# Splitting a second layer's output weights ahead of time and parking them in device memory

## The chip, the cores and the metric

The kernel runs on one core of a Trainium2 chip. The metric is device time in microseconds of one launch; the time before is a median of three runs. The profile shows one further execution of the same program.

## The reference, cut to what matters

Two batches of 12-head attention (448 positions, 64 wide) with a mixing of heads before and after the softmax, then two dense layers on the 896 tokens that come out of it. `w_out` of the second layer is the matrix whose handling changes.

```python
scores = scale * q @ k.T ; scores = einsum('bhij,hg->bgij', scores, w_pre)
attn   = softmax(scores) ; attn   = einsum('bhij,hg->bgij', attn, w_post)
x = (attn @ v) laid out as (896, 768)
h = x @ moe_w_in                       # 768 -> 2048
x = (h * clip(h + 3, 0, 6) / 6) @ moe_w_out      # 2048 -> 768
h = x @ moe2_w_in
P = a0 + a1*h + a2*h**2 + a3*h**3
Q = 1 + |b0|*|h| + |b1|*h**2
out = (P / (Q + 1e-6)) @ moe2_w_out
```

The weights arrive as float64. They are turned into float32 on the chip, and every product is made of three float32r matmuls (high times high, high times low, low times high), so each operand is split into a high part (`h`) and a low part (`l`).

## The kernel before, in words

**Attention, 0 to about 240 us.** The queries go in eight chunks (four for each batch) of 12, 12, 12 and 9 steps; a step handles ten query rows of all heads. The order of each step is written out by hand: `premix` (three matmuls into `M`, then a maximum on VectorE and an exponential on ScalarE), `postmix` of two steps before (eight matmuls into `A`), and at set steps either `scores` of the next chunk (twelve matmuls) or `av_unit`, attention times values of the chunk before (32 matmuls into `X` in a step that has two units). The tables `SST`, `QST` and `AVST` say which step of a chunk holds what. `scores` are evicted into `stg` tiles and moved ("spread") into the layout of the mix, `full`, by twelve DMAs a head pair's worth at a time (line 250). GpSimd splits each `full` slice (`gsplit`, lines 287 and 289) two steps before it is used, and the first split of a chunk needs every spread of that chunk. `load_v` (line 132) fetches values three or four head pairs ahead into four `vraw` buffers. All these DMAs are issued by SyncE (SP), in program order. The keys of batch two (`load_k`, line 126; three DMAs of 448 KB) and their splits (`k_prep`: a ScalarE cast on line 234, a VectorE subtraction on line 235 a step later) are put into chunk 2, the third. `kraw` and `stg` share the five buffers of the tag `raw`.

**Layer 1, about 240 to 475 us.** Written in order, but from here on a planner in the framework reorders the instructions of each engine by its own cost model, within the dependencies. Meanwhile ten slices of the second layer's `w_in` are converted and parked in device memory (`pre`, line 713), to be fetched back in layer 2 (line 398).

**Layer 2, first half, about 475 to 644 us.** For each of 16 slices `f` of the 2048 hidden units: `gemm_in` for tokens 0 to 383 (part 0) and for tokens 384 to 895 (part 1), six steps of three matmuls each; the rational function `act2` on part 0 and its split into `g0`; then the product of slice `f - 1` with `w_out` (`gemm_out0`, 18 matmuls) into six PSUM banks. Part 1 of a slice is kept in `g1[f]`: with `act2` done at once for four slices (`f % 4 == 3`), only copied for the twelve others (`late_f`). A slice of `w_out` is loaded as raw float64 (`wraw`, two buffers), converted (`to_f32`: ScalarE line 419, VectorE lines 421, 423 and 427) into its own place in `wo2`, which holds all 16, and split (`wh`, `wl`, lines 451 and 452).

**Layer 2, second half, about 644 to 720 us.** Part 1 times `w_out`, 16 slices of 24 matmuls (four blocks of 128 tokens, two halves of the columns): 384 matmuls. `prep(i)` splits `g1[f]` (lines 773 and 774) and splits the slice of `w_out` once more, out of `wo2` (lines 844 and 845). `act2` of the twelve late slices runs here as well. The last two slices are kept for the end (`TAIL`), where each bank is finished, evicted and stored.

Of the kernel before, what the change touches and what calls it, by code (L numbers as in the profile page):

```python
# [7 lines left out]
F32 = mybir.dt.float32  # L8
F32R = mybir.dt.float32r
I32 = mybir.dt.int32  # L10
AF = mybir.ActivationFunctionType
ALU = mybir.AluOpType
# [14 lines left out]
NP = H // 2  # L27
# [21 lines left out]
def fused_kernel(  # L49
# [15 lines left out]
    nc = tc.nc  # L65
# [30 lines left out]
    PRE2 = list(range(2, 12))  # L96
    dram = ctx.enter_context(tc.tile_pool(name="dram", bufs=1, space=bass.MemoryType.DRAM))
    pre = {f: dram.tile([128, KD * 128], F32, name=f"pre{f}") for f in PRE2}

    xp = tc.alloc_tile_pool(name="xp", bufs=1)  # L100
    x1p = tc.alloc_tile_pool(name="x1p", bufs=1)
# [22 lines left out]
    def load_k(b, m):  # L124
        t = front.tile([128, 2, S], F32, tag="raw", bufs=5, name=f"kraw{b}_{m}")
        nc.sync.dma_start(out=t, in_=k[b, :, 2 * m : 2 * m + 2])
        kraw[(b, m)] = t
# [102 lines left out]
    def k_prep(b, hp):  # L230
        src = kraw[(b, hp // 2)][:, hp % 2, :]
        hi, lo = kst[:, 0, hp, :], kst[:, 1, hp, :]
        preps.append([
            lambda: nc.scalar.activation(out=hi, in_=src, func=AF.Copy),
            lambda: nc.vector.tensor_tensor(out=lo, in0=src, in1=hi.bitcast(F32), op=ALU.subtract),
        ])
# [151 lines left out]
        if f >= GLAG:  # L388
            units.append(("out2", f - GLAG, 0))
    raws, spl = {}, {}  # L390
    wo2 = []
    ucur = [0, 0]

    def load_unit(u, eng=nc.sync):
# [37 lines left out]
    def split_pieces(u):  # L432
        t, n = raws.pop(u)
        n *= 128
        if u[0] == "in2" and u[1] in pre:
            w = t
        else:
            if u[0] == "out2":
                if not wo2:
                    wo2.append(pools["gp2"].tile([128, KF, DM], F32, name="wo2"))  # L440
                w = wo2[0][:, u[1], :]
            else:
                w = pools["late"].tile([128, KD * 128], F32, tag="wf", bufs=2, name="wf")[:, :n]
            yield from to_f32(t, n, w)
        hv = pools["late"].tile([128, KD * 128], F32R, tag="wh", bufs=3, name="wh")[:, :n]
        lv = pools["late"].tile([128, KD * 128], F32R, tag="wl", bufs=3, name="wl")[:, :n]
        if u[0] in ("in1", "out1"):
            nc.gpsimd.tensor_scalar(out=hv, in0=w, scalar1=1.0, scalar2=0.0, op0=ALU.mult, op1=ALU.add)  # L448
            nc.gpsimd.tensor_tensor(out=lv, in0=w, in1=hv.bitcast(F32), op=ALU.subtract)  # L449
        else:  # L450
            nc.scalar.activation(out=hv, in_=w, func=AF.Copy)
            nc.vector.tensor_tensor(out=lv, in0=w, in1=hv.bitcast(F32), op=ALU.subtract)  # L452
        if u[0] != "out2":
            hv, lv = (x.rearrange("p (a b) -> p a b", b=128) for x in (hv, lv))
        spl[u] = (hv, lv)

# [14 lines left out]
    def advance(i):  # L471
        load_units(i + 2)
        split_units(i + 1)
# [35 lines left out]
    def gemm_in(p, hp, w):  # L509
        t0, t1 = PARTS[p]  # L510
        wh, wl = w
        for c in range(KD):
            yield mm3(hp[:, : t1 - t0], wh[:, c, :], wl[:, c, :], XH[:, c, t0:t1], XL[:, c, t0:t1], c == 0, c == KD - 1)
# [5 lines left out]
    def run(g):  # L519
        for _ in g:  # L520
            pass
# [35 lines left out]
    for C, (b, r0, n, G) in enumerate(chunks):  # L557
# [3 lines left out]
        def add(units, steps):  # L561
            for i, u in enumerate(units):
                sched.setdefault(steps[i * len(steps) // len(units)], []).append(u)
# [3 lines left out]
        if C + 2 < len(chunks):  # L567
            add([lambda: q_prep(C + 2, 0, NP // 2), lambda: q_prep(C + 2, NP // 2, NP)], QST[G])
        if C == NCH - 2:
            add([lambda m=m: load_k(1, m) for m in range(3)], [4, 5, 6])  # L570
            add([lambda h=h: k_prep(1, h) for h in range(NP - 1)], [8, 8, 9, 10, 11])
        if C == NCH - 1:
            add([lambda: k_prep(1, NP - 1)], [0])
        if C > 0:
            add([lambda h=h: av_unit(C - 1, h) for h in range(1, H, 2)], [("av", a) for a in (AVST[G] if nxt is not None else AVLAST)])

# [173 lines left out]
    def bank2(tag, name):  # L750
        return pm.tile([128, 512], F32, tag=tag, name=name)
# [36 lines left out]

    acc0 = []
    g0, g1 = {}, {}  # L790
    late_f = [f for f in range(KF) if f % 4 != 3]

    def gemm_out0(f):
        w = spl.pop(("out2", f, 0))
# [5 lines left out]
    for f in range(KF):  # L800
        advance(ui)
        w = spl.pop(("in2", f, 0))
        tags = (f"a{2 - f}0", f"a{2 - f}1") if f < GLAG else ("h0", "h1")
        g1[f] = gp.tile([128, P1], F32, tag=f"g1_{f}", name=f"g1_{f}")
        hp = bank2(tags[0], f"h2_{f}_0")
        run(gemm_in(0, hp, w))
        t1 = tm("t1", P0)
        act2(hp[:, :P0], t1, P0)
        g0[f] = tuple(gp.tile([128, P0], F32R, tag="g0" + x, bufs=GLAG + 1, name=f"g0{x}{f}") for x in "hl")
        last = split(t1, *g0[f])  # L810
        hp = bank2(tags[1], f"h2_{f}_1")
        run(gemm_in(1, hp, w))
        if f in late_f:
            nc.scalar.activation(out=g1[f], in_=hp[:, :P1], func=AF.Copy)
        else:
            act2(hp[:, :P1], g1[f], P1)
        ui += 1
        if f >= GLAG:
            advance(ui)
            if f == GLAG:  # L820
                acc0 += [[bank2(f"a{t}{i}", f"acc{t}{i}") for i in range(2)] for t in range(NB0)]
            gemm_out0(f - GLAG)
            ui += 1
    for f in range(KF - GLAG, KF):
        advance(ui)
        gemm_out0(f)
        ui += 1


    flat = [x.rearrange("p c t -> p (c t)") for x in (XH, XL)]  # L830
    NSL = 4
    order = [f for f in range(KF) if f not in late_f] + late_f
    gs, ws = {}, {}

    def prep(i):
        if i >= KF:
            return
        f, sl = order[i], i % NSL
        gs[f] = tuple(x[:, sl * P1 : sl * P1 + P1] for x in flat)
        split(g1[f], *gs[f])  # L840
        w0 = NSL * P1 + sl * DM
        ws[f] = tuple(x[:, w0 : w0 + DM] for x in flat)
        hv, lv = ws[f]
        nc.scalar.activation(out=hv, in_=wo2[0][:, f, :], func=AF.Copy)
        nc.vector.tensor_tensor(out=lv, in0=wo2[0][:, f, :], in1=hv.bitcast(F32), op=ALU.subtract)

    with tc.issue_after(last[0].ins), tc.issue_after(last[1].ins):
        prep(0)
        prep(1)
    for t in range(NB0):  # L850
        o = gp.tile([TB, DM], F32, tag="o", bufs=3, name=f"o0_{t}")
        for i in range(2):
            put(acc0[t][i], t, i, o, i)
        nc.sync.dma_start(out=out[t * TB : t * TB + TB, :], in_=o)
    tags = [("h0", "h1")] + [(f"a{t}0", f"a{t}1") for t in range(NB0)]
    acc1 = [[bank2(tags[t][i], f"acc1{t}{i}") for i in range(2)] for t in range(NB1)]
    TAIL = 2
    for i in range(KF - TAIL):
        with tc.issue_after(last[0].ins), tc.issue_after(last[1].ins):
            prep(i + 2)  # L860
            if i < len(late_f):
                f = late_f[i]
                act2(g1[f], g1[f], P1)
        f = order[i]
        for t in range(NB1):
            for j in range(2):
                gemm_out(acc1[t][j], t, j, gs[f], ws[f], i == 0, False)
    for t in range(NB1):
        row = P0 + t * TB
        o = gp.tile([TB, DM], F32, tag="o", bufs=3, name=f"o1_{t}")  # L870
# [61 lines left out]
```

## Time and profile before

| | |
|---|---|
| median of three runs | 725.36 us (724.59 to 727.18) |
| the profiled execution: its time, its span | 725.5 us, 723.8 us |
| TensorE busy | 697.5 us, 96% of the span |
| VectorE, ScalarE, GpSimd busy | 571.9, 425.5, 257.4 us |
| mean granted TensorE clock | 0.990 of full speed |
| DMA, mean | 135 GB/s, 97.65 MB |

The span is the time from the first to the last instruction of the profiled execution; its own time is 1.7 us longer. Matmuls overlap one another in the records, so a busy TensorE is not yet a TensorE at its peak: their starts tell more than their durations.

### The profile page before, as it was taken

The page shows a single profiled execution, that of the slowest core. Times are in us where ns is not written, and L with a number is a line of the kernel's source. Part 1 is how long each engine was busy: PE and PEld are TensorE (multiplying, and loading weights), DVE is VectorE, ACT ScalarE, POOL GpSimd, SP SyncE. Part 2 cuts the span into 40 slices and gives each one's busy share as a digit, 9 for nine tenths or more (in the row PEclk, how much of TensorE's full clock was granted, in tenths as well). Part 3 has the DMA queues.
Part 4 walks back from the last instruction along what each step waited for, and adds up shares of the span by engine and source line. Part 5 has one row for each costly group of instructions (what it writes and reads, how often), then busy time and mean ns, then how long its engine had stood idle before and what let it go on. Part 6 is the DMA issues. An engine that isn't in the chain of part 4 may idle for free.

```text
span 723.8 us, 12235 instructions
## 1 busy us (share of the span) xinstructions
PE 697.5 (96%) x4457; PEld 620.3 (86%) x4457; DVE 571.9 (79%) x947; ACT 425.5 (59%) x869; POOL 257.4 (36%) x255
## 2 busy tenths in 40 slices
PE   5999989999999999999999999999999999999986
PEld 3779878898888888989888888889899999999976
DVE  5566656665657589899988777899998789789996
ACT  4687868777788443434322221166766677589872
POOL 1787745877778234332444444300000000000000
PEclk8899999999999999999999999999999999999999
DMA  6635565556384354454355455354444222010002
GB/s 193 232 99 163 166 163 177 162 145 190 98 247 144 113 171 130 153 157 150 128 173 172 144 182 180 110 196 155 174 140 144 66 92 89 39 65 1 1 1 88
DMA packets 66333, 97.65 MB, mean 135 GB/s; under 512 B 5532, under 2 KB 54496, under 8 KB 66272
## 3 DMA queue, kind: packets, MB, share of 16 engines
q1 hardware_dynamic: 65920, 96.48, 42.5%
q8 instruction: 35, 0.57, 0.3%
q10 hardware_dynamic: 288, 0.37, 0.1%
q0 software_dynamic: 64, 0.01, 0.1%
q14 instruction: 26, 0.21, 0.1%
HBM read 70.81 MB, written 6.68 MB: 107 GB/s over the span
## 4 chain that ended last, share of the span: by engine, by line
PE 43%; DVE 37%; DMA 10%; issue 5%; ACT 3%; POOL 2%; SPq 0%; ACTq 0%; POOLq 0%; DVEq 0%
PE A L334 8%; DVE wf L423 6%; DVE wf L427 6%; PE X L354 5%; PE h L378 4%; PE h L379 4%; PE sc L268 4%; PE h L380 4%; DMA pre<-wf 4%; DVE gl L539 4%; DVE wf L421 3%; PE M L299 3%; DMA vraw<-in_v_dram 3%; PE acc L379 2%; PE M L301 2%
## 5 line engine op out<-in xcount | busy, mean ns | idle before, releaser
L378 PE MATMUL h<-xh,wh 128*128 128x512 f32 (+1 forms) x384 | 141.7, 369 | 0.6 <-DVE u L766 0.6
L380 PE MATMUL h<-xh,wl 128*128 128x512 f32 (+1 forms) x384 | 140.8, 367 | 0.7 <-DVE wl L452 0.7
L379 PE MATMUL h<-xl,wh 128*128 128x512 f32 (+1 forms) x384 | 140.6, 366 | 0.0
L289 POOL TENSOR_TENSOR sl<-full,sh 120x448 fp32r<-120x448 f32 x89 | 103.0, 1157 | 7.4
L303 DVE TENSOR_REDUCE st<-M 120x1 f32<-120x448 f32 x90 | 56.0, 623 | 57.0 <-PE M L301 56.7
L334 PEld LDWEIGHTS A<-wr,e 120*112 120x112 f32 x720 | 86.4, 176 | 7.7 <-ACT wr L318 3.4
L334 PE MATMUL A<-wr,e 120*112 120x120 f32 x720 | 88.9, 266 | 1.6 <-ACT wr L318 1.6
L419 ACT ACTIVATE wf<-wraw 128x768 f32<-128x768 f32 (+1 forms) x40 | 34.1, 864 | 88.8 <-DMA pre<-wf 56.2
L305 ACT ACTIVATE e<-M,st 120x448 f32<-120x448 f32 x90 | 57.1, 635 | 46.5 <-DVE st L303 46.2
L448 POOL TENSOR_SCALAR wh<-wf 128x768 fp32r<-128x768 f32 (+1 forms) x34 | 32.7, 961 | 138.8 <-DVE wf L427 126.3
L380 PEld LDWEIGHTS h<-xh,wl 128*128 128x128 f32 x384 | 72.1, 188 | 10.1 <-DVE wl L452 1.0
L378 PEld LDWEIGHTS h<-xh,wh 128*128 128x128 f32 x384 | 72.1, 188 | 9.0 <-DVE u L766 1.0
L379 PEld LDWEIGHTS h<-xl,wh 128*128 128x128 f32 x384 | 72.1, 188 | 8.0
L287 POOL TENSOR_SCALAR sh<-full 120x448 fp32r<-120x448 f32 x89 | 54.0, 606 | 62.1 <-PE M L300 35.7
L380 PE MATMUL y<-gh,wl 128*128 128x384 f32 x192 | 70.3, 366 | 0.7 <-POOL wl L449 0.7
L378 PE MATMUL y<-gh,wh 128*128 128x384 f32 x192 | 70.4, 366 | 0.0
L379 PE MATMUL y<-gl,wh 128*128 128x384 f32 x192 | 70.2, 366 | 0.0
L449 POOL TENSOR_TENSOR wl<-wf,wh 128x768 fp32r<-128x768 f32 (+1 forms) x34 | 67.6, 1989 | 2.8
L538 ACT ACTIVATE gh<-g 128x384 fp32r<-128x384 f32 (+1 forms) x32 | 18.6, 580 | 60.3 <-DVE g L536 60.0
L338 ACT ACTIVATE at<-A 112x480 f32<-112x480 f32 x90 | 52.2, 580 | 1.8 <-PE A L334 1.8
L421 DVE TENSOR_SCALAR wf<-wf 128x768 int32<-128x768 int32 (+1 forms) x50 | 33.6, 671 | 21.9 <-ACT wf L419 21.9
L299 PE MATMUL M<-sh,wp_h 120*120 120x448 f32 x90 | 41.4, 460 | 5.7 <-DVE sh L287 5.7
(116 smaller groups left out, 1589.5 us busy)
## 6 DMA issues: line engine op xcount, KB each, us to landing
wraw<-in_moe_w_out_dram SPq DMA_DIRECT2D x28, 768.0 KB
wraw<-in_moe_w_in_dram SPq DMA_DIRECT2D x22, 768.0 KB
full<-stg SPq DMA_DIRECT2D x60, 210.0 KB
vraw<-in_v_dram SPq DMA_DIRECT2D x42, 224.0 KB
wpre<-in_moe_w_in_dram SPq DMA_DIRECT2D x10, 768.0 KB
pre<-wf SPq DMA_DIRECT2D x10, 384.0 KB
wf<-pre SPq DMA_DIRECT2D x10, 384.0 KB
full<-stg SPq DMA_DIRECT2D x24, 157.5 KB
```

Source lines behind the costliest of these rows:

```text
L287: eng.tensor_scalar(out=sh[:r], in0=s[:r], scalar1=1.0, scalar2=0.0, op0=ALU.mult, op1=ALU.add)
L289: return eng.tensor_tensor(out=sl[:r], in0=s[:r], in1=sh[:r].bitcast(F32), op=ALU.subtract)
L299: nc.tensor.matmul(mt[:r, :S], lhsT=a[:r, :r], rhs=sh[:r], start=True, stop=False)
L303: nc.vector.tensor_reduce(out=st[:r, 0:1], in_=mt[:r, :S], op=ALU.max, axis=AX.X, negate=True)
L305: nc.scalar.activation(out=e[:r], in_=mt[:r, :S], func=AF.Exp, bias=st[:r, 0:1], accum_out=st[:r, 1:2])
L334: nc.tensor.matmul(av[:, jc], lhsT=e[:r, jc * JP : (jc + 1) * JP], rhs=wr[:r, :, :rr], start=True, stop=True)
L338: lambda: nc.scalar.activation(out=at[C][:, :, :, c0 : c0 + rr], in_=av, func=AF.Copy)
L378: nc.tensor.matmul(o, lhsT=wh, rhs=mh, start=first, stop=False)
L379: nc.tensor.matmul(o, lhsT=wh, rhs=ml, start=False, stop=False)
L380: nc.tensor.matmul(o, lhsT=wl, rhs=mh, start=False, stop=last)
L421: nc.vector.tensor_scalar(out=wi, in0=wi, scalar1=3, scalar2=None, op0=ALU.logical_shift_left)
L449: nc.gpsimd.tensor_tensor(out=lv, in0=w, in1=hv.bitcast(F32), op=ALU.subtract)
```

## The change

1. In the second layer's first half each slice of `w_out` is converted into a `wf` buffer (two of them, shared with `w_in`; `wo2` is gone), split once, used, and both parts are stored in device memory (`wsp`). In the second half they are fetched back (`fetch`) into seven pairs of buffers, six pairs of which are asked for before that half begins. `prep` no longer splits weights.
2. The four slices whose `act2` on part 1 is done at once are 2, 5, 8 and 11 instead of 3, 7, 11 and 15.
3. For slice 0 the first five of six steps of both parts go ahead of the sixth of part 0. At the end of the first half the products of the first two slices for the first block of tokens go ahead of the last `gemm_out0`, and those of the third behind it.
4. In chunk 2 of the attention the three key loads go to steps 6, 7 and 9 instead of 4, 5 and 6; the key splits to steps 9, 10, 10 and 11 and to steps 0 and 1 of the next chunk.

```diff
+    wsp = {f: [dram.tile([128, DM], F32, name=f"w2{x}{f}") for x in "hl"] for f in range(KF)}
...
-            if u[0] == "out2":
-                if not wo2:
-                    wo2.append(pools["gp2"].tile([128, KF, DM], F32, name="wo2"))
-                w = wo2[0][:, u[1], :]
-            else:
-                w = pools["late"].tile([128, KD * 128], F32, tag="wf", bufs=2, name="wf")[:, :n]
+            w = pools["late"].tile([128, KD * 128], F32, tag="wf", bufs=2, name="wf")[:, :n]
...
-        if u[0] != "out2":
+        if u[0] == "out2":
+            for d, x in zip(wsp[u[1]], (hv, lv)):
+                nc.sync.dma_start(out=d, in_=x.bitcast(F32))
+        else:
...
-            add([lambda m=m: load_k(1, m) for m in range(3)], [4, 5, 6])
-            add([lambda h=h: k_prep(1, h) for h in range(NP - 1)], [8, 8, 9, 10, 11])
+            add([lambda m=m: load_k(1, m) for m in range(3)], [6, 7, 9])
+            add([lambda h=h: k_prep(1, h) for h in range(4)], [9, 10, 10, 11])
         if C == NCH - 1:
-            add([lambda: k_prep(1, NP - 1)], [0])
+            add([lambda h=h: k_prep(1, h) for h in range(4, NP)], [0, 1])
...
-    late_f = [f for f in range(KF) if f % 4 != 3]
+    early_f = [2, 5, 8, 11]
+    late_f = [f for f in range(KF) if f not in early_f]
...
+        hps = [bank2(tags[p], f"h2_{f}_{p}") for p in range(2)] if f == 0 else [bank2(tags[0], f"h2_{f}_0")]
+        gemms = [gemm_in(p, hp, w) for p, hp in enumerate(hps)]
+        if f == 0:
+            for g in gemms:
+                for _ in range(KD - 1):
+                    next(g)
...
-        w0 = NSL * P1 + sl * DM
-        ws[f] = tuple(x[:, w0 : w0 + DM] for x in flat)
-        hv, lv = ws[f]
-        nc.scalar.activation(out=hv, in_=wo2[0][:, f, :], func=AF.Copy)
-        nc.vector.tensor_tensor(out=lv, in0=wo2[0][:, f, :], in1=hv.bitcast(F32), op=ALU.subtract)
+    def fetch(i):
...
+        ws[f] = tuple(gp.tile([128, DM], F32R, tag="ws" + x, bufs=NWS, name=f"ws{x}{f}") for x in "hl")
+        for d, x in zip(wsp[f], ws[f]):
+            nc.sync.dma_start(out=x.bitcast(F32), in_=d)
+    for i in range(NWS - 1):
+        fetch(i)
+    prep(0)
+    prep(1)
     with tc.issue_after(last[0].ins), tc.issue_after(last[1].ins):
-        prep(0)
-        prep(1)
+        prep(2)
...
+    products(0, 0)
+    products(1, 0)
+    for f in range(KF - GLAG, KF):
+        advance(ui)
+        gemm_out0(f)
+        ui += 1
+    products(2, 0)
+    fetch(NWS - 1)
...
     for i in range(KF - TAIL):
...
+            if i + 2 >= AHEAD:
+                prep(i + 2)
...
+        for t in range(i < AHEAD, NB1):
+            products(i, t)
+        fetch(i + NWS)
```

## Rows read from the trace of the kernel before

**Rows 1.** The page's first part: busy time, share, instructions of an engine.
```profile
PE 697.5 (96%) x4457; PEld 620.3 (86%) x4457; DVE 571.9 (79%) x947; ACT 425.5 (59%) x869; POOL 257.4 (36%) x255
```

**Rows 2.** All waits of TensorE, whole run: total us, times, longest us.
```profile
PE acc L379 <- DVE xl L845: 4.9, 4, 2.2
PE X L354 <- DMA vraw<-in_v_dram: 2.9, 1, 2.9
...
PE h L380 <- DVE wl L452: 0.7, 1, 0.7
PE h L378 <- DVE u L766: 0.6, 1, 0.6
```

**Rows 3.** Busy time by stretch: window, length, engines' busy us, PEclk, DMA share, GB/s.
```profile
85.00:107.00 22.00, 19.11 (x187) 16.94 (x185) 12.07 (x32) 15.04 (x41) 12.62 (x15) 0.92 0.71 183
...
475.80:520.00 44.20, 43.51 (x221) 39.66 (x222) 43.32 (x68) 31.86 (x54) 0.00 (x0) 1.00 0.51 178
...
600.00:644.50 44.50, 44.50 (x233) 41.25 (x232) 37.69 (x58) 28.59 (x49) 0.00 (x0) 1.00 0.10 36
644.50:682.00 37.50, 37.50 (x216) 37.08 (x216) 37.50 (x59) 34.97 (x59) 0.00 (x0) 1.00 0.08 32
682.00:719.50 37.50, 31.82 (x171) 29.08 (x170) 34.10 (x53) 22.84 (x38) 0.00 (x0) 1.00 0.08 28
```

**Rows 4.** Timeline of TensorE, end of chunk 2: start, us, instruction, idle before.
```profile
90.69 0.47 PE L299 MATMUL M<-sh,wp_h 120*120 120x448 f32 x1
...
95.55 0.47 PE L299 MATMUL M<-sh,wp_h 120*120 120x448 f32 x1
...
101.57 3.07 PE L354 MATMUL X<-at,vraw 112*64 112x120 f32 x32 [2.89 <-DMA vraw<-in_v_dram]
104.57 0.73 PE L299 MATMUL M<-sh,wp_h 120*120 120x448 f32 x1
```

**Rows 5.** Granted clock right behind that wait, columns as in rows 3.
```profile
102.00:105.40 3.40, 3.40 (x30) 3.04 (x27) 0.17 (x1) 0.77 (x2) 0.90 (x1) 0.50 0.30 77
```

**Rows 6.** Timeline of SP's queue ahead of that wait: start, us of issuing.
```profile
85.81 0.95 SPq L126 DMA_DIRECT2D kraw<-in_k_dram  x2
86.86 3.36 SPq L250 DMA_DIRECT2D full<-stg  x4
90.33 0.89 SPq L126 DMA_DIRECT2D kraw<-in_k_dram  x1
91.27 1.04 SPq L132 DMA_DIRECT2D vraw<-in_v_dram  x2
```

**Rows 7.** Timelines of GpSimd and ScalarE in the same steps.
```profile
98.81 0.60 POOL L287 TENSOR_SCALAR sh<-full 120x448 fp32r<-120x448 f32 x1 [3.80 <-DMA vraw<-in_v_dram]
...
100.47 0.56 ACT L234 ACTIVATE xh<-kraw 128x448 fp32r<-128x448 f32 x1
```

**Rows 8.** Groups of VectorE's instructions, 640 to 724 us: busy us, mean ns.
```profile
L845 DVE TENSOR_TENSOR xl<-wo,xh 128x768 fp32r<-128x768 f32 x16 | 15.1, 942 | 0.0
L774 DVE TENSOR_TENSOR xl<-g,xh 128x512 fp32r<-128x512 f32 x16 | 10.8, 675 | 0.0
L762 DVE SCALAR_TENSOR_TENSOR y<-h,pb,y 128x512 f32<-128x512 f32 x13 | 9.6, 736 | 0.0
...
L769 DVE SCALAR_TENSOR_TENSOR g<-y,u 128x512 f32<-128x512 f32 x13 | 8.8, 674 | 0.0
```

**Rows 9.** Timeline of TensorE: two slices' starts in the first half, last matmul.
```profile
620.38 0.34 PE L378 MATMUL h<-xh,wh 128*128 128x384 f32 x1
...
630.88 0.34 PE L378 MATMUL h<-xh,wh 128*128 128x384 f32 x1
...
719.31 0.34 PE L380 MATMUL acc<-xh,xl 128*128 128x384 f32 x1
```

**Rows 10.** The chain of waits, layer 1: one store of 384 KB, issue to landing.
```profile
265.51 2.77 DMA pre<-wf
```

**Rows 11.** Waits in SP's queue, 475 to 645 us: total us, times, longest.
```profile
SPq L398 <- DVE wl L452: 39.8, 10, 7.8
```

More of the change, by code (lines that the diff above doesn't have):

```diff
@@ L390, in fused_kernel @@
     raws, spl = {}, {}
-    wo2 = []
     ucur = [0, 0]
@@ L804, in fused_kernel @@
         g1[f] = gp.tile([128, P1], F32, tag=f"g1_{f}", name=f"g1_{f}")
-        hp = bank2(tags[0], f"h2_{f}_0")
-        run(gemm_in(0, hp, w))
+        hps = [bank2(tags[p], f"h2_{f}_{p}") for p in range(2)] if f == 0 else [bank2(tags[0], f"h2_{f}_0")]
[4 more added lines that the diff above has]
+                    next(g)
+        hp = hps[0]
+        run(gemms[0])
         t1 = tm("t1", P0)
@@ L810, in fused_kernel @@
         last = split(t1, *g0[f])
-        hp = bank2(tags[1], f"h2_{f}_1")
-        run(gemm_in(1, hp, w))
+        if f == 0:
+            hp = hps[1]
+            run(gemms[1])
+        else:
+            hp = bank2(tags[1], f"h2_{f}_1")
+            run(gemm_in(1, hp, w))
         if f in late_f:
@@ L823, in fused_kernel @@
             ui += 1
[L824 to L827, printed above, removed]
     flat = [x.rearrange("p c t -> p (c t)") for x in (XH, XL)]
-    NSL = 4
-    order = [f for f in range(KF) if f not in late_f] + late_f
+    NSL, NWS = 4, 7
+    order = early_f + late_f
     gs, ws = {}, {}
@@ L840, in prep, with products @@
         split(g1[f], *gs[f])
-        w0 = NSL * P1 + sl * DM
-        ws[f] = tuple(x[:, w0 : w0 + DM] for x in flat)
-        hv, lv = ws[f]
-        nc.scalar.activation(out=hv, in_=wo2[0][:, f, :], func=AF.Copy)
-        nc.vector.tensor_tensor(out=lv, in0=wo2[0][:, f, :], in1=hv.bitcast(F32), op=ALU.subtract)
-    with tc.issue_after(last[0].ins), tc.issue_after(last[1].ins):
-        prep(0)
-        prep(1)
+    def fetch(i):
+        if i >= KF:
+            return
+        f = order[i]
+        ws[f] = tuple(gp.tile([128, DM], F32R, tag="ws" + x, bufs=NWS, name=f"ws{x}{f}") for x in "hl")
[3 more added lines that the diff above has]
+        fetch(i)
+    AHEAD = 3
+    prep(0)
+    prep(1)
+    with tc.issue_after(last[0].ins), tc.issue_after(last[1].ins):
+        prep(2)
+    acc1 = [[bank2(x, f"acc10{j}") for j, x in enumerate(("h0", "h1"))]]
+    def products(i, t, last=False):
+        f = order[i]
+        for j in range(2):
+            gemm_out(acc1[t][j], t, j, gs[f], ws[f], i == 0, last)
+    products(0, 0)
[6 more added lines that the diff above has]
+    fetch(NWS - 1)
     for t in range(NB0):
@@ L854, in fused_kernel @@
         nc.sync.dma_start(out=out[t * TB : t * TB + TB, :], in_=o)
-    tags = [("h0", "h1")] + [(f"a{t}0", f"a{t}1") for t in range(NB0)]
-    acc1 = [[bank2(tags[t][i], f"acc1{t}{i}") for i in range(2)] for t in range(NB1)]
+    acc1 += [[bank2(f"a{t}{j}", f"acc1{t + 1}{j}") for j in range(2)] for t in range(NB0)]
     TAIL = 2
@@ L859, in fused_kernel @@
         with tc.issue_after(last[0].ins), tc.issue_after(last[1].ins):
-            prep(i + 2)
+            if i + 2 >= AHEAD:
+                prep(i + 2)
             if i < len(late_f):
@@ L863, in fused_kernel @@
                 act2(g1[f], g1[f], P1)
[L864 to L867, printed above, removed]
+        for t in range(i < AHEAD, NB1):
+            products(i, t)
+        fetch(i + NWS)
     for t in range(NB1):
```

## The prediction

> **What bounds the kernel now.** I read the busy times first: TensorE is busy 96% of the span, and no other engine is above 79% [rows 1]. So the end moves only where TensorE is kept waiting, or is slowed. The second view, TensorE's own waits over the whole run, has few that a change in the named places could touch: 4.9 us for `xl` of line 845, which is the second split of `w_out`; 2.9 us, once, for a load of values; and 0.7 and 0.6 us in layer 2 [rows 2]. Matmuls overlap in the records, so these idle times are lower bounds, and I size each from starts instead.
>
> The windows by stage say where VectorE takes over. Up to 644.5 us of layer 2 TensorE is fully busy or within 0.7 us of it in each stretch. In 644.5 to 682 VectorE works 37.50 of 37.5 us, and in 682 to 719.5 TensorE falls to 31.82 of 37.5 [rows 3]. The second half of layer 2 is bound by VectorE and TensorE pays for it late, when the work prepared ahead is used up.
>
> **Term 1: the second half without a second split.** This half has 384 matmuls. While TensorE still runs freely it does 216 in 37.5 us [rows 3], 0.1736 us each, so 384 need 66.7 us. The half begins at 644.5 and its last matmul starts at 719.31 [rows 3, 9], so the last one ends its turn at 719.5: 75.0 us. What can be had is 75.0 - 66.7 = 8.3 us. Is VectorE really out of the way? It loses 16 subtractions of 942 ns, 15.1 us. It also loses the `act2` of slice 15, which was done at once and fell into the start of this half; that is now one of the copied slices, twelve as before, with the fourth at-once slice moved to 11. What stays for each copied slice is six operations of 674 to 736 ns, taken as 6 x 705 = 4.23 us, and one split of 675 ns [rows 8]: 4.9 us, twelve times 58.9, with the four early splits (2.7) and bank copies (three, 1.7 us by the same size of operation) 63.3 us. That is under 66.7 us, and it begins before TensorE's half, at about 640 us. The durations also overlap a little (59 instructions in 37.5 us [rows 3] are 0.64 us each where the rows say 0.67 to 0.94). So TensorE sets this half, with VectorE close behind. I take 8.0 us, with bounds of 6 (VectorE's order costs two microseconds) and 8.3.
>
> The weights must now come by DMA: 2 x 384 KB a slice, six slices ahead of the half and ten in it. One transfer of 384 KB took 2.77 us from issue to landing [rows 10]. Even one after the other, ten pairs take 10 x 2 x 2.77 = 55.4 us from 645 on, to 700 us; the last slices are wanted at 644.5 + 14 x 24 x 0.1736 = 702.8. It holds at the worst rate, and DMA is busy only 0.08 of this stretch now [rows 3]. I cost it at nothing; if it were one slice late at the end, 4.2 us.
>
> **Term 2: the keys of batch two.** Two steps, the second with 32 value matmuls, take 95.55 - 90.69 = 4.86 us from mix to mix; the next two, of the same kind and the last of chunk 2, take 104.57 - 95.55 = 9.02 us [rows 4]. The difference is 4.2 us. It is made of 2.89 us of waiting for values [rows 4] and of the granted clock that followed the wait, 0.50 (1.2 of 2.4 GHz) from 102.0 to 105.4 [rows 5]. SP's queue shows why: two key loads, four spreads, the third key load, and then the values, issued at 91.27 and first used at 101.57 [rows 6, 4]. Also GpSimd waited until 98.81 to split the first slice of the next chunk [rows 7]; its releaser is named as values, but that instruction reads `full`, so it is the spreads that came late, behind two key loads. With the change the spreads have no key load in front and the values have one instead of three. Two key loads are 0.92 MB; at the 183 GB/s of this stretch [rows 3] that is 5.0 us. The values are then there at 96.5 us, where TensorE wants them at 101.57 - 2.89 = 98.7. Two microseconds of slack: the whole 4.2 us, bounds 1 and 4.6 (the slow clock also stretched the next step a little).
>
> The keys themselves come later. The second load stands behind the two value loads: 96.5, plus 1.2 us for the other value load (224 KB) and 2.5 us for itself at the same rate, is 100.2. Its first cast on ScalarE is due in the last step of chunk 2, where the row of before has a cast at 100.47 [rows 7]. That is just in time, and ScalarE executes in order, so exponentials and evictions are queued behind this cast. I take nothing, up to 2 us if it comes late.
>
> **Term 3: the first half of layer 2.** One slice takes 630.88 - 620.38 = 10.50 us of TensorE [rows 9]. The split and conversion of `w_out` were already here; only their buffer changes. New are 32 stores of 384 KB and six pairs of fetches, 17.3 MB in 168.7 us, 103 GB/s more. At the start DMA had a share of 0.51 at 178 GB/s [rows 3], so 0.80; later far less. That fits. The fourth at-once `act2`, 4.23 us of VectorE, moves in here, and the first comes one slice sooner, into a stretch where VectorE works 43.32 of 44.2 us [rows 3]. At-once slices already cost TensorE 0.6 us there (the wait for line 766, [rows 2]). With only two `wf` buffers, conversions can no longer run several slices ahead, so that the last five slices (11 with its `act2`, and 12 to 15, whose `w_in` is not parked) must be nearly served as they come. I take a loss of 1.5 us, from 0 to 5, the upper end being one `act2` not hidden at all and 0.8 for the start.
>
> A page of the Trainium skill speaks against this part. The trace has SP holding back the loads of parked `w_in` for 39.8 us in ten waits without TensorE noticing [rows 11, 2]. "DMA: Bandwidth & Descriptors", section on the anatomy of one DMA, says that DMA engines do not wait on semaphores: any wait happens on the issuing sequencer before dispatch. By that rule each of the 32 stores, which waits for ScalarE or VectorE, holds up every load behind it in SP's queue, and the sum would come out as in rival D, 727.6 us; by the row such waits are free and it stays as below.
>
> **Term 4: slice 0 and the products put forward.** The change of layer shows one wait, 0.7 us for `wl` [rows 2], and that weight is needed by the third matmul in either order. At the change of halves there is no wait to fill. So 0, with 0.7 as the gain if the planner's order happens to shift.
>
> **The sum.** 725.5 (the profiled execution) - 8.0 - 4.2 + 1.5 = 714.8. The profiled execution is 0.1 above the median of the runs, so 714.7 us. Its own range, from the terms: 725.4 - 8.3 - 4.6 - 0.7 = 711.8, to 725.4 - 7 - 4.2 + 4 = 718.2.
>
> **The rivals.**
> - A, both stalls go, as above: 714.7. For it: both are measured waits whose cause is removed, not covered.
> - B, the keys' wait only changes place: the second load lands late, ScalarE stands on its cast and the chunk starts late by 3 us of the 4.2. 725.4 - 8.0 - 1.2 + 1.5 = 717.7. For it: the estimate above has no slack. Against: ScalarE idles some microseconds right after.
> - C, the first half turns VectorE-bound: the five last slices and the four at-once ones lose 5 to 7 us together. 725.4 - 8.0 - 4.2 + 6 = 719.2. For it: VectorE's 43.32 of 44.2 us; against: 37.69 of 44.5 at the other end [rows 3].
> - D, the other side: stores in SP's queue keep loads back, every slice. It decides from (8.0 + 4.2) / 16 = 0.76 us a slice; one store's time, 2.77 us [rows 10], unhidden in half of the slices would be 22 us, and at 0.9 us a slice, just past that point, the time is 725.4 - 12.2 + 16 x 0.9 = 727.6. Against: loads are asked for more than a slice of 10.5 us ahead, and rows 11.
> - E, second half not freed: the fetches or VectorE's order cost what the split did. 725.4 - 4.2 + 1.5 = 722.7.
>
> **How the numbers follow.** A 0.62, B 0.11, C 0.12, D 0.07, E 0.08. About 0.3% (2.2 us) is what a measurement can tell from no change, so faster is below 723.2. A, B and C are, 0.85, and half of E: 0.89. The same: the other half of E and a little of D, 0.06. Slower: 0.05. The range takes A with B and C: 711.5 to 720.5, which leaves out D, E and the rims.
>
> **What would show it.** In the changed profile: TensorE's matmuls of the second half 0.174 us apart throughout and no wait for a weight's split there; no wait of TensorE on values near 100 us, no half clock from 102 us, and the last two steps of chunk 2 together about 4.9 us long; GpSimd's split of the next chunk starting near 95.5. Wrong would be: new waits of TensorE for `wl` or `wh` in 475 to 640 us, a ScalarE cast of keys with idle time before it, SP waits on stores with loads late behind them, or a fetched weight that TensorE waits for.

## The result, and the profile after

The changed kernel takes 717.92 us (median of four runs, 716.96 to 718.5) beside 724.98 us of the kernel before (723.74 to 727.18): a ratio of 0.9906, interval [0.9879, 0.9932]. The forecast was 714.7 us, range 711.5 to 720.5. The profiled execution took 718.42 us, its span is 716.7.

The span fell by 7.05 us. Cut at starts of matmuls in the two timelines, it falls into these pieces (steps are counted through all chunks, so chunk 3 is steps 36 to 44; "last `h`" is the last matmul with `w_in` of layer 2, so the last piece holds 36 matmuls of the first half and the 384 of the second):

| stage | before | after | change |
|---|---|---|---|
| start to step 14 (first loads) | 49.02 | 49.70 | +0.7 |
| the last two steps of chunk 2, 34 and 35 (term 2) | 9.02 | 4.85 | -4.2 |
| the last two steps of chunk 3, 43 and 44 | 6.98 | 8.24 | +1.3 |
| end of chunk 3 to the first `h` of layer 2 | 345.83 | 346.32 | +0.5 |
| first `h` to last `h` (terms 3 and 4) | 163.40 | 165.69 | +2.3 |
| last `h` to last `acc` (term 1) | 81.29 | 73.62 | -7.7 |

The rest is unchanged within 0.1 us. On the page, VectorE and ScalarE have each lost 16 instructions and 14.0 and 12.8 us of work (compare [rows 1]); TensorE lost 2.6 us of busy time:

```profile
PE 694.9 (97%) x4457; PEld 618.9 (86%) x4457; DVE 557.9 (78%) x931; ACT 412.7 (58%) x853; POOL 257.5 (36%) x255
```

From all waits of TensorE in the changed kernel, as in [rows 2]:

```profile
PE X L355 <- DMA vraw<-in_v_dram: 1.4, 1, 1.4
PE h L381 <- DVE wl L447: 1.3, 2, 0.9
...
PE y L381 <- POOL wl L444: 1.2, 2, 0.8
PE acc L380 <- DVE wl L447: 0.9, 1, 0.9
PE h L380 <- DVE xl L736: 0.5, 1, 0.5
PE acc L381 <- DVE xl L772: 0.4, 1, 0.4
PE sc L269 <- DVE xh L236: 0.2, 1, 0.2
```

The 4.9 us for line 845 are gone with the line. A wait for values is still there, half as long, but now at the end of chunk 3 (124.85 us) and not of chunk 2. Four waits are new: `acc` for a `wl`, `h` for `xl` of line 736 (the last slice of the activations that come out of layer 1), a second `h` for `wl`, and `sc` for the split of the keys (line 236, at 104.19 us).

The windows, columns as in [rows 3]; the first is the stretch in which [rows 5] showed 0.50:

```profile
102.00:105.40 3.40, 3.20 (x24) 2.37 (x23) 3.20 (x8) 2.70 (x9) 1.63 (x3) 1.00 0.66 213
472.90:520.00 47.10, 45.63 (x230) 41.12 (x230) 40.99 (x64) 31.13 (x53) 0.00 (x0) 1.00 0.59 193
520.00:560.00 40.00, 40.00 (x210) 37.11 (x209) 33.34 (x52) 25.11 (x42) 0.00 (x0) 1.00 0.61 206
560.00:600.00 40.00, 40.00 (x208) 36.94 (x207) 37.71 (x59) 29.11 (x48) 0.00 (x0) 1.00 0.66 225
600.00:642.00 42.00, 40.67 (x205) 36.45 (x205) 38.78 (x59) 25.79 (x43) 0.00 (x0) 1.00 0.73 246
642.00:680.00 38.00, 37.65 (x217) 37.32 (x216) 38.00 (x63) 34.24 (x60) 0.00 (x0) 1.00 0.54 189
680.00:712.40 32.40, 32.40 (x189) 32.28 (x187) 21.28 (x35) 13.41 (x23) 0.00 (x0) 1.00 0.24 84
```

The clock near 102 us is full. The second half keeps TensorE busy to the end, while VectorE, busy 38.00 of 38.00 us in its first part, falls to 21.28 of 32.4 in the last. And both ends of the first half now have idle time: 47.10 - 45.63 = 1.5 us and 42.00 - 40.67 = 1.3 us, where the stretches of [rows 3] had 0.7 and 0.0.

### The profile page after: what moved, and what is told of

It reads as the page before. It is cut to its first block, busy times and chain, and to the rows that moved or that the text cites. A ratio compares the mean times of both kernels' runs of the same rounds, so it can differ in the third digit from the quotient of the medians.

```text
span 716.7 us, 12362 instructions
## 1 busy us (share of the span) xinstructions
PE 694.9 (97%) x4457; PEld 618.9 (86%) x4457; DVE 557.9 (78%) x931; ACT 412.7 (58%) x853; POOL 257.5 (36%) x255
## 4 chain that ended last, share of the span: by engine, by line
PE 55%; DVE 28%; DMA 7%; issue 4%; ACT 4%; POOL 2%; SPq 0%; ACTq 0%; POOLq 0%; DVEq 0%
PE A L335 8%; DVE wf L427 6%; DVE wf L423 6%; PE acc L381 5%; PE acc L380 5%; PE acc L379 5%; PE h L380 5%; PE h L379 5%; PE h L381 5%; PE X L355 5%; PE sc L269 4%; DMA pre<-wf 4%; DVE gl L537 4%; DVE wf L421 3%; PE M L300 3%
## 5 line engine op out<-in xcount | busy, mean ns | idle before, releaser
L419 ACT ACTIVATE wf<-wraw 128x768 f32<-128x768 f32 (+1 forms) x56 | 48.7, 878 | 98.4 <-DMA pre<-wf 56.6
L423 DVE SCALAR_TENSOR_TENSOR wf<-wraw,icst,wf 128x768 int32<-128x768 int32 (+1 forms) x56 | 62.2, 1110 | 1.0
L421 DVE TENSOR_SCALAR wf<-wf 128x768 int32<-128x768 int32 x66 | 42.6, 645 | 24.9 <-ACT wf L419 24.7
L427 DVE SCALAR_TENSOR_TENSOR wf<-wraw,icst,wf 128x768 int32<-128x768 int32 (+1 forms) x56 | 57.1, 1022 | 0.6
```

What stands on the lines that cost most here:

```text
L421: nc.vector.tensor_scalar(out=wi, in0=wi, scalar1=3, scalar2=None, op0=ALU.logical_shift_left)
L423: nc.vector.scalar_tensor_tensor(out=wi, in0=hw, scalar=icst[:, 0:1], in1=wi, op0=ALU.bitwise_and, op1=ALU.bitwise_or)
L427: nc.vector.scalar_tensor_tensor(out=wi, in0=lw, scalar=icst[:, 1:2], in1=wi, op0=ALU.logical_shift_right, op1=ALU.bitwise_or)
```

## The experiments

Every whole time carries the first loads: step 14 begins between 47.6 and 50.6 us from execution to execution, whatever the kernel. So stages are compared, from the trace of each run, and whole times only where there are several runs. (Line numbers shift by a few from kernel to kernel: the splits of `w_out` are lines 446 and 447 in the changed kernel.)

**Part 4 alone** (the keys, put into the kernel before):

```diff
-            add([lambda m=m: load_k(1, m) for m in range(3)], [4, 5, 6])
-            add([lambda h=h: k_prep(1, h) for h in range(NP - 1)], [8, 8, 9, 10, 11])
+            add([lambda m=m: load_k(1, m) for m in range(3)], [6, 7, 9])
+            add([lambda h=h: k_prep(1, h) for h in range(4)], [9, 10, 10, 11])
...
-            add([lambda: k_prep(1, NP - 1)], [0])
+            add([lambda h=h: k_prep(1, h) for h in range(4, NP)], [0, 1])
```

> The kernel before with the key loads and key splits alone at their new steps. Theory: the two steps at the end of chunk 2 take 4.86 us instead of 9.02, but the value load at the end of chunk 3, which had no slack before, is now waited for by about 1.3 us, so the last value matmul of the attention starts 2.5 to 3 us sooner and the time falls by as much, to 722.3. Rival: the wait at the end of chunk 3 comes from the stores and fetches or from chance, and the whole 4.2 us arrive at the end: 720.8.

Measured: 722.09 us (nine runs) beside 724.87 (eighteen), 2.8 us less by the medians; the ratio, 0.9942 [0.9919, 0.9964], stands for 4.2 us, with 2.6 to 5.9 as its interval. The last two steps of chunk 2 take 4.85 us; those of chunk 3 take 7.58, where 6.98 stood: 3.6 us less together in the profiled executions. The gain is real, and part of it comes back one chunk later, as in the changed kernel. The long times go as well: the eighteen runs of before lie between 723.55 and 730.06 us, the nine of this kernel between 721.16 and 722.59.

**All but part 4** (the same lines turned round, in the changed kernel):

> The changed kernel with the key loads and splits at their old steps. Theory: the parts add up, so it loses what the keys alone bring, 2.5 to 3 us, and runs at 720.7; layer 2 is as in the changed kernel (73.6 us from the last matmul of the first product to the last of all). Rival, the parts hide each other: within 1 us of the changed kernel.

Measured: 719.33 us (716.91 to 723.56, ten runs), ratio 0.9919 [0.9895, 0.9943], 1.4 us above the changed kernel's median, though the two intervals overlap, and with the old order of the keys the wide spread is there too. In the profiled execution, the fastest of the ten, the wait that part 4 removes is only 1.78 us long, and the clock does not fall behind it. From the timeline of TensorE and the windows:

```profile
100.57 1.86 PE L355 MATMUL X<-at,vraw 112*64 112x120 f32 x32 [1.78 <-DMA vraw<-in_v_dram]
```
```profile
102.00:105.40 3.40, 3.40 (x33) 2.64 (x28) 2.13 (x4) 2.23 (x6) 2.43 (x3) 1.00 0.71 210
```

So the stall of [rows 4] is not one number. Over the profiled executions with the old order of the keys the last two steps of chunk 2 take 9.02, 8.74 and 6.70 us; over all with the new order 4.85. The other place varies too: the last two steps of chunk 3 take 6.81 to 7.13 us with the old order (three executions), 6.81 to 8.24 with the new (ten, `AVST` as it was), 7.0 and 7.5 us in the mean. By these means part 4 saves 8.15 - 4.85 = 3.3 and gives back 0.5: 2.8 us, what the medians gave alone. Three executions are few for such a mean, and no long run of the old order was profiled.

**The values asked for sooner**, to take that return away:

```diff
-    AVST = {12: [7, 7, 9, 9, 11, 11], 9: [5, 5, 7, 7, 8, 8]}
+    AVST = {12: [7, 7, 9, 9, 11, 11], 9: [3, 3, 6, 6, 8, 8]}
```

> The changed kernel with the value units of a 9-step chunk at steps 3, 3, 6, 6, 8, 8 instead of 5, 5, 7, 7, 8, 8, so that the last value loads are issued two steps sooner, between spreads and not behind all twelve. Theory (the loads queue behind the spreads on SP): the step into chunk 4 falls from 4.84 to 3.4 us, no wait of TensorE on values there, 1.2 to 1.4 us gained. Rival (DMA bandwidth is short there, whatever the order): the wait stays or moves to the spreads, and less than 0.5 us is gained.

Measured: 716.0 us (714.31 to 717.39, four runs), ratio 0.9864 [0.9831, 0.9897], but by stage nothing was won: from step 36 to step 84 it takes 115.45 us, the changed kernel 115.51. TensorE no longer waits for values; it waits for the split of the next chunk, since that needs the spreads, which now have two value loads between them. GpSimd and TensorE:

```profile
123.99 0.56 POOL L288 TENSOR_SCALAR sh<-full 120x448 fp32r<-120x448 f32 x1 [5.00 <-DMA vraw<-in_v_dram]
```
```profile
125.83 0.46 PE L302 MATMUL M<-sl,wp_h 120*120 120x448 f32 x1 [0.55 <-POOL sl L290]
```

The rival held: at this place twelve spreads and the values share the same transfers, and what goes first makes the other late. The lower time of the profiled execution (716.73 against 718.42 us) is that of the first loads (step 14 at 48.88 us, against 49.70) and of layer 2, where the first half took 164.94 us against 165.69 with the very same instructions.

**No second split at all**: the kernel before without lines 844 and 845. The second half then multiplies with whatever stands in the buffers that the split would have filled; no store and no fetch is added.

```diff
...
-        hv, lv = ws[f]
-        nc.scalar.activation(out=hv, in_=wo2[0][:, f, :], func=AF.Copy)
-        nc.vector.tensor_tensor(out=lv, in0=wo2[0][:, f, :], in1=hv.bitcast(F32), op=ALU.subtract)
```

> The kernel before with the second split of the output weights left out (lines 844 and 845; the second half multiplies with whatever stands in those buffers, so its products are not the reference's). No store, no fetch. Theory: VectorE's 16 subtractions are all of the second half's loss, so the 384 matmuls take 66.7 to 67.3 us and the time falls by 7.7 to 8.3 us, to about 717; the first half stays at 163.4 us. The changed kernel's first half is 2.3 us longer, which would then be the price of the stores, the fetches and the two buffers. Rival: act2 keeps VectorE the bound and only 4 to 5 us come.

Measured: 717.19 us (four runs), ratio 0.9889 [0.9851, 0.9926]. From the last `h` to the last `acc` it takes 72.86 us, 8.4 less than before, and the first half is unchanged at 163.64. TensorE is busy without a gap, and VectorE, with the split gone, has 8 us to spare at the end:

```profile
643.00:680.00 37.00, 37.00 (x215) 37.00 (x215) 36.94 (x61) 32.30 (x56) 0.00 (x0) 1.00 0.09 33
680.00:710.20 30.20, 30.20 (x176) 30.10 (x174) 21.73 (x35) 14.44 (x24) 0.00 (x0) 1.00 0.11 38
```

420 matmuls at 0.1736 us are 72.9 us: this is the floor, and the changed kernel stands 0.7 us above it. What the split cost is settled, and so is about what the new way costs: 0.7 us here and some 2 us in the first half.

**Slice 0 in its old order**, in the changed kernel:

```diff
-        hps = [bank2(tags[p], f"h2_{f}_{p}") for p in range(2)] if f == 0 else [bank2(tags[0], f"h2_{f}_0")]
+        hps = [bank2(tags[p], f"h2_{f}_{p}") for p in range(2)] if False else [bank2(tags[0], f"h2_{f}_0")]
...
-        if f == 0:
+        if False:
             for g in gemms:
                 for _ in range(KD - 1):
...
-        if f == 0:
+        if False:
             hp = hps[1]
             run(gemms[1])
```

> The changed kernel with slice 0 in the order of before (all six steps of part 0, then part 1). Theory: putting the first five steps of both parts ahead gained nothing and made the planner put the last slice of the activations off behind other work of VectorE, which TensorE now waits 0.7 us for (line 736); with the old order this wait is gone and the 0.9 to 1.1 us for the weight's low part stay, first half 165.0 us instead of 165.7. Rival: the old order uncovers a longer wait for the activations, over 1 us, and the first half gets longer.

Measured: 727.04 us in one run, and a first half of 175.70 us, 10.0 more than the changed kernel. My theory (that this order is worth next to nothing) fell. TensorE reaches the sixth step of part 0 and waits for the last slice of the activations, and the granted clock is 0.50 behind that wait:

```profile
475.61 0.34 PE L381 MATMUL h<-xh,wl 128*128 128x384 f32 x1
478.36 0.44 PE L379 MATMUL h<-xh,wh 128*128 128x384 f32 x1 [2.41 <-DVE xh L735]
```
```profile
480.00:483.40 3.40, 3.40 (x10) 2.62 (x9) 3.09 (x7) 2.27 (x5) 0.00 (x0) 0.50 0.94 330
```

Near the end of the half it waits again, three times for a high part of `w_in` (one row of the waits from 470 to 646 us):

```profile
PE h L379 <- ACT wh L446: 4.0, 3, 2.0
```

The wait for the activations is new. In the kernel before, VectorE casts this slice (`xh<-y`) 2.2 us after layer 2 begins, in the changed kernel 6.0 us after (474.62 and 472.96 are the beginnings). ScalarE shows why: the conversion of a slice of `w_out` stands in front of the eviction of the activations, and waits until a `wf` buffer is free. On VectorE the rest of that conversion then stands in front of the cast. In the kernel before both come behind the activations. The kernel before, ScalarE and then VectorE:

```profile
475.78 0.96 ACT L736 ACTIVATE y<-y 128x384 f32<-128x384 f32 x2
476.62 0.92 ACT L419 ACTIVATE wo<-wraw 128x768 f32<-128x768 f32 x1
```
```profile
476.78 0.35 DVE L737 CAST xh<-y 128x384 fp32r<-128x384 f32 x1
```

The changed kernel, ScalarE and then VectorE:

```profile
475.44 0.91 ACT L419 ACTIVATE wf<-wraw 128x768 f32<-128x768 f32 x1 [1.03 <-DVE wl L447]
476.25 0.96 ACT L734 ACTIVATE y<-y 128x384 f32<-128x384 f32 x2
```
```profile
478.03 1.02 DVE L427 SCALAR_TENSOR_TENSOR wf<-wraw,icst,wf 128x768 int32<-128x768 int32 x1
478.96 0.35 DVE L735 CAST xh<-y 128x384 fp32r<-128x384 f32 x1
```

So the change makes the activations late and its part 3 covers that: two parts of one edit, each of which is misread alone.

**Conversion buffers of its own for `w_out`** (two, beside the two that `w_in` keeps):

```diff
-            w = pools["late"].tile([128, KD * 128], F32, tag="wf", bufs=2, name="wf")[:, :n]
+            if u[0] == "out2":
+                w = pools["gp2"].tile([128, DM], F32, tag="wo", bufs=2, name="wo")
+            else:
+                w = pools["late"].tile([128, KD * 128], F32, tag="wf", bufs=2, name="wf")[:, :n]
```

> The changed kernel with two conversion buffers of the output weights' own, beside the two of the input weights. Theory S (two shared buffers let conversions run no further ahead): the waits of TensorE for weights near 626 and 631 us (1.0, 0.2 and 0.6 us) go, first half 164.0 us. Theory T (late raw loads, since stores and early fetches share the DMA engines; one took 7.6 us there where 4.5 is usual): the waits stay within 0.3 us, first half 165.4 or more.

> The same kernel as own_buffers (the changed kernel with two conversion buffers of its own for w_out), now timed. Theory (the changed kernel pays for the buffers that w_in and w_out share, and for nothing else in layer 2): first half 163 us, second half 73 us, and since the changed kernel has 165.7 and 73.6, some 3 us less than it: 715 us, ratio to the kernel before 0.987. Rival (the one look at 711.6 was a lucky start-up of the first loads and the first half's gain was chance): 717.5 to 718 us, ratio 0.990, with the first half over 165 us.

Measured: 711.61 us in one run; in four more 713.03 us (711.27 to 714.4) beside 725.7 (nine), ratio 0.9823 [0.9801, 0.9845]. The first half takes 163.18 and 163.14 us, as before the change, and the last piece 72.93 twice, the floor. The waits of the changed kernel in layer 2 are gone but for the one at the change of layer (0.8 us, as before the change). TensorE's waits, VectorE's cast and the windows in the profile of the four runs:

```profile
PE h L381 <- DVE wl L450: 0.8, 1, 0.8
...
PE acc L381 <- DVE g0l L775: 0.2, 1, 0.2
```
```profile
474.38 0.35 DVE L738 CAST xh<-y 128x384 fp32r<-128x384 f32 x1
```
```profile
600.00:638.70 38.70, 38.70 (x200) 35.44 (x199) 34.48 (x53) 22.31 (x39) 0.00 (x0) 1.00 0.64 226
638.70:676.00 37.30, 37.30 (x216) 37.30 (x215) 36.14 (x60) 33.70 (x58) 0.00 (x0) 1.00 0.53 180
```

The cast is back at 2.2 us after the beginning of layer 2 (472.18). The theory held, and this version beats both kernels. By stages it is 2.5 + 0.7 = 3.2 us better than the changed kernel in its profile, and 2.8 us by the mean first half of the three executions with shared buffers (165.23 us, below); the two intervals put the difference of the whole times between 2.5 and 9.5 us.

**Own buffers, slice 0 in its old order:**

> Own conversion buffers, with slice 0 in the old order (part 0 to its end, then part 1). Theory (with shared buffers the last slice of the activations is split late, 6.0 us after layer 2 begins against 2.2 before, because VectorE's split queues behind conversions that wait for a shared buffer; the order put forward covers just that): with buffers of their own the split is early again, no wait of 2.6 us at the start, no half clock, first half 163 to 164.5 us. Rival (the late split comes from the stores or from the planner's other order, not from the buffers): a wait over 1.5 us within the first 8 us of layer 2 and a first half over 168 us.

Measured: a first half of 163.33 us (whole time 715.36, one run), no wait at the start beyond the one for `wl`, full clock. The cast:

```profile
475.02 0.35 DVE L738 CAST xh<-y 128x384 fp32r<-128x384 f32 x1
```

It comes 2.2 us after the beginning (472.87). The lateness is that of the shared buffers, and with it gone the order of slice 0 is worth 0.2 us, the zero that I had given it.

**The six early pairs of fetches behind the last raw load**, first in the changed kernel, then with own buffers:

```diff
...
-        eng.dma_start(out=t[:, : n * 256].rearrange("p (a b) -> p a b", b=256), in_=src)
+        rawins[0] = eng.dma_start(out=t[:, : n * 256].rearrange("p (a b) -> p a b", b=256), in_=src)
...
-    for i in range(NWS - 1):
-        fetch(i)
+    while ucur[0] < len(units):
+        load_units(len(units))
+    with tc.issue_after(rawins[0].ins):
+        for i in range(NWS - 1):
+            fetch(i)
```

> The changed kernel with the six early fetches queued on SP behind the last raw load of the first half. Theory T (DMA contention makes raw loads late): raw loads near 616 us land in 5 to 6 us, the waits near 626 and 631 us fall under 0.5 us together, first half 164.2 us; the fetches then fall into 625 to 645 us and the second half may wait 0 to 2 us for its first weights. Theory S (buffers): the waits stay, 1.5 us or more.

> Own conversion buffers, and the six early pairs of fetches asked for behind the last raw load of w_out. Theory (what the late fetches gave by themselves, 1.4 us of the first half, was the same loss that the shared buffers make, so the two do not add up): the same as own_timed within 1 us, first half 163 us. Rival (contention of fetches with the last raw loads is a loss of its own): first half 161.5 to 162 us and a time 1 to 1.5 us below own_timed.

Measured: 713.77 us (one run) with a first half of 164.28, 1.4 less than the changed kernel, though only 0.7 to 0.8 less than two other executions of the same layer 2; with own buffers 713.24 us (five runs), ratio 0.9827 [0.9803, 0.9851], first half 162.96. So the fetches seem to meet the last raw loads where the conversions are already short of time (one execution), but it is the same loss as that of the buffers, not a second one: with own buffers it makes 0.2 us.

**The four at-once slices back at 3, 7, 11 and 15:**

```diff
-    early_f = [2, 5, 8, 11]
+    early_f = [3, 7, 11, 15]
```

> The changed kernel with act2 done at once for slices 3, 7, 11 and 15 as before, instead of 2, 5, 8 and 11. If the earlier slices are what costs the first half its 2.3 us, it falls to 163.5 to 164 us; the second half then has the act2 of slice 15 in front of it on VectorE and may begin 1 to 3 us late. If the price is DMA or buffers, the first half stays within 0.5 us of 165.7 and the second half gets no shorter.

Measured: 717.1 us (one run), first half 166.23, last piece 74.30: no better in either. The place of the at-once `act2` is not what the first half pays for.

**Each store issued twice**, the second time to other device memory that nothing reads:

```diff
+    wsp2 = {f: [dram.tile([128, DM], F32, name=f"w3{x}{f}") for x in "hl"] for f in range(KF)}
...
+            for d, x in zip(wsp2[u[1]], (hv, lv)):
+                nc.sync.dma_start(out=d, in_=x.bitcast(F32))
```

> The changed kernel with every store of a split w_out slice issued a second time, to other device memory: 32 DMAs and 12.6 MB more, which nothing reads. Theory (stores only load the DMA engines; the waits of SP's queue are free as long as loads are asked for a slice ahead): first half 166 to 169 us, the growth lying at 610 to 635 us where raw loads, stores and fetches meet. Rival (the rule weighed in the prediction: each store in SP's queue holds loads back): at least 0.76 us for each of 16 slices, first half 178 us or more, with waits of TensorE for wh or wl spread over all slices.

Measured: 727.36 us (one run), first half 177.27 us, 11.6 more than the changed kernel. Neither expectation fits: it is far more than the 169 of the theory, but not spread over the slices. TensorE's waits in layer 2, the windows around 600 us and two pieces of the chain of waits:

```profile
PE h L380 <- ACT wh L447: 6.1, 6, 2.8
PE h L382 <- DVE wl L448: 2.5, 3, 1.1
```
```profile
596.00:602.00 6.00, 3.18 (x19) 2.83 (x17) 5.42 (x10) 4.89 (x9) 0.00 (x0) 1.00 0.98 369
602.00:608.80 6.80, 4.87 (x14) 3.69 (x13) 6.68 (x10) 2.19 (x4) 0.00 (x0) 0.50 0.25 83
```
```profile
583.20 7.07 DMA wraw<-in_moe_w_in_dram
...
593.25 4.99 DMA wraw<-in_moe_w_out_dram
```

By the starts of its matmuls TensorE loses 2.2 us in four waits between 540 and 590 us. Then, where raw `w_in` has to be loaded again, DMA is busy 0.98 of a stretch, the raw loads take 7.07 and 4.99 us one after the other, TensorE is busy 3.18 of 6.0 us, and the clock is 0.50 in the 6.8 us behind. Doubled stores make one place break, the one with no reserve. SP's waits for what the first set of stores writes out did not grow, 38.3 us (below) against 39.4 in the changed kernel:

```profile
SPq L451 <- ACT wh L447: 25.6, 16, 4.3
SPq L451 <- DVE wl L448: 12.7, 16, 1.1
```

That speaks against the rival's way. Whether the queue's order or the transfers themselves are late there this run does not tell, since it doubles both.

## Why the prediction was right or wrong

**Term 1, the second half: right.** 7.7 us against 8.0. The floor of 0.1736 us a matmul is reached without the split (8.4 us), the changed kernel stops 0.7 us short of it with a wait for `xl` of line 772 in the stretch where VectorE works 38.00 of 38.00 us; this is the "two microseconds of VectorE's order" of the lower bound, at a third. No matmul waits for a fetched weight, as forecast. Rival E is out.

**Term 2, the keys: right in mechanism, too large by some 1.4 us.** The 4.85 us for the two steps are exactly what was forecast, the clock stays at full speed, and TensorE waits for the split of the keys for 0.2 us only, so rival B is out where I had put it. One sign was missed: GpSimd's split of the next chunk starts at 97.00 us and not near 95.5, after 1.30 us of idle time where it was 3.80, and TensorE does not wait for it:

```profile
97.00 0.56 POOL L288 TENSOR_SCALAR sh<-full 120x448 fp32r<-120x448 f32 x1 [1.30 <-DMA vraw<-in_v_dram]
```

Two things were mis-sized. The 9.02 us that I read were the longest of three executions with that order of the keys, one each of three kernels (the mean is 8.15); and TensorE, sooner at the end of chunk 3, finds the values behind that chunk's spreads. The first cannot be seen in one profile, but the second could be worked out from SP's queue: I followed the values of chunk 2 and not the next ones. In the changed kernel SP issues twelve spreads and then the values, and TensorE waits for the first of them (TensorE and then SP's queue):

```profile
118.40 0.44 PE L300 MATMUL M<-sh,wp_h 120*120 120x448 f32 x1
...
124.85 1.86 PE L355 MATMUL X<-at,vraw 112*64 112x120 f32 x32 [1.35 <-DMA vraw<-in_v_dram]
126.64 0.47 PE L300 MATMUL M<-sh,wp_h 120*120 120x448 f32 x1
```
```profile
105.92 12.95 SPq L251 DMA_DIRECT2D full<-stg  x12
118.97 8.10 SPq L133 DMA_DIRECT2D vraw<-in_v_dram  x6
```

"The values are then there" holds for chunk 2 only. The term is 2.8 us by the medians of part 4 alone and by the means of the stages, inside its bounds of 1 and 4.6; by the ratio of part 4 alone it would be the forecast 4.2, so how much too large it was is not settled.

**Term 3, the first half: right in sign, 2.3 us in this profile and 1.8 in the mean for 1.5, and for one of its three reasons.** All but part 4 and the values asked for sooner have the same instructions in layer 2 as the changed kernel, and first halves of 165.05 and 164.94 us: with 165.69 the mean is 165.23, against 163.48 for three executions of the old way (163.40, 163.39, 163.64). TensorE's wait of `acc` for `wl` is 0.86 us long here and 0.33 in the other two. So the 2.3 us are the longest of three draws, as the 9.02 us were, and the forecast was nearer than the table says. "With only two `wf` buffers, conversions can no longer run several slices ahead" is what the run with own buffers shows: the loss goes to nothing. The at-once slices cost nothing that the one run shows, and the transfers, as far as two runs tell, cost something only where conversions are short of time. The late place is readable in the changed kernel: the last raw load of `w_in` is issued at 616.28 us, 22.4 before the last `h`, and ScalarE stands idle for it; with own buffers the same load is issued at 609.11, 26.2 before. ScalarE in the changed kernel:

```profile
623.99 0.89 ACT L419 ACTIVATE wf<-wraw 128x768 f32<-128x768 f32 x1 [4.32 <-DMA wraw<-in_moe_w_in_dram]
```

Rival C (5 to 7 us) is out: TensorE is fully busy from 520 to 600 us. What I had named as a sign of being wrong, new waits for `wl` before 640 us, did appear, of 0.9 and 0.4 us.

**The rule that was weighed, and rival D.** SP's queue waits 39.4 us in 32 waits for what the stores write out, first rows, and 58.3 us with own buffers, second rows. That the waiting is done by the issuing sequencer is what the Trainium skill says ("DMA: Bandwidth & Descriptors", anatomy of one DMA), and the trace agrees.

```profile
SPq L450 <- ACT wh L446: 21.8, 16, 6.2
SPq L450 <- DVE wl L447: 17.6, 16, 2.4
```
```profile
SPq L453 <- ACT wh L449: 42.7, 14, 7.0
...
SPq L453 <- DVE wl L450: 15.6, 16, 1.5
```

But the kernel whose SP waits longer for its stores has the shorter first half, 163.1 us against 165.7. These waits are free here, where the loads are asked for early enough; rival D is out for this number of stores. The run with twice as many shows only that a second set, by its place in the queue or by its transfers, is more than the reserve.

**Term 4, the order of slice 0: the step that failed.** "The change of layer shows one wait ... So 0" reads the kernel before, where the activations were early. The change itself makes them 3.8 us later, and the order put forward leaves 0.5 us of that to TensorE. Without it the changed kernel loses 10.0 us, more than its whole gain: some 4 at the start (the wait and the slow clock), the rest in the waits near 612 to 640 us, whose growth I did not trace further. I had costed part 3 apart from parts 1 and 2; its price depends on them. That the sum held is luck in this place: a loss of 10 us from the shared buffers that term 3 did not see was hidden by an order that term 4 put at nothing. The products put forward at the change of halves were not tried alone; the run without a second split has none of them and reaches the floor too.

**What lay outside the terms**: 0.5 us between chunk 3 and layer 2 (waits of `y` for `wl` of GpSimd, 1.2 us after) and 0.7 us of first loads. The first was not traced to a cause. With the terms as measured the sum is 725.0 - 7.7 - 2.8 + 2.3 + 0.5 = 717.3, beside the median of 717.92; of the 2.6 us by which 714.7 was exceeded at this sum, 1.4 are term 2, 0.8 term 3, 0.3 term 1, 0.5 lay outside, and 0.4 go the other way, the base being 725.0 here and 725.4 there. With 1.8 us for term 3, its mean, the sum is 716.8, and 1.1 us up to the median are left without a term, less than the first loads vary by. The "own range" of the sum was too narrow at its top: 718.2 took 7, 4.2 and 4 us where the terms had given 6, 1 and 5 as their bounds, which makes 723.4.

## What to carry to other kernels

A wait read from one profile is one draw: where it hangs on transfers in a queue, follow the next thing in the same queue after the wait is gone, and expect part of it back there. When a buffer becomes shared, cost it at the place where the two users meet under time pressure (here the change of layer and the last slices), and not by its number in the steady state; two more buffers were worth some 3 us where the whole change gave 7. And cost the parts of an edit together: a reordering that does nothing in the kernel before can be what hides the lateness that its sister part makes.

## What the runs showed of the hardware that was not expected

- The first 14 steps, with identical instructions in every kernel here, end anywhere from 47.6 to 50.6 us (47.64 and 49.16 in two executions of one kernel); a gain below 3 us is not read from one whole time.
- Behind single waits of TensorE of 2.89, 2.82 and 2.41 us the granted clock was 0.50 (1.2 GHz) for 3.4 us and more; behind waits of 1.78 and 1.35 us it stayed at 1.00 (2.4 GHz). So the wait of 2.89 us made two steps 9.02 us long and that of 1.78 only 6.70: 1.1 us more of waiting, 2.3 us more of time. The length of the wait alone does not decide: at the same place of the second half, with the same instructions, a wait of 2.19 us in the kernel before left the clock at 1.00 and one of 2.22 us with part 4 alone was followed by 0.51, first and second row:

```profile
707.20:710.60 3.40, 3.40 (x20) 3.40 (x21) 3.40 (x6) 2.00 (x3) 0.00 (x0) 1.00 0.01 2
```
```profile
703.80:707.20 3.40, 3.40 (x11) 3.40 (x12) 3.40 (x6) 1.98 (x3) 0.00 (x0) 0.51 0.01 2
```

- VectorE, with 16 instructions less, is as busy as before in the first part of the second half (38.00 of 38.00 us): it runs on with work that was later before, and the relief is seen only at the end, 21.28 of 32.4 us against 34.10 of 37.5 [rows 3].
